# Softmax attention with decay, then two mixture layers, on one core: q and k rounded for both heads at once, row sums cut at other columns, and the conversions' ScalarE and GpSimd work queued a half step later

## The chip, the cores and the metric

The kernel runs on one core of a Trainium2 chip. A core has five engines that run side by side, each with its own queue that is worked off in order: TensorE (PE; its weight loads are listed as PEld), VectorE (DVE), ScalarE (ACT), GpSimd (POOL), and SyncE (SP), which here issues every DMA. Where an instruction needs what another engine makes, it waits on a semaphore, and all that stands behind it in its queue waits too. The metric is the device time of one execution in microseconds; less is better.

## The reference, cut to what matters

Four batches, eight heads, 576 tokens, 64 values a head; all in float32.

```
scores = q @ k.T / 8                                    # per batch and head, 576 x 576
decay  = cumsum(log f)[:, None] - cumsum(log f)[None]
scores = where(causal, -1e9, scores + decay)
attn   = exp(scores - max(scores, -1))
attn   = attn / (sum(attn, -1) + 1e-9)
x = attn @ v                                            # 2304 tokens x 512
h = x @ w_in;  x = (h * sigmoid(h)) @ w_out             # 512 -> 2048 -> 512
logits = x @ phi                                        # 2304 x 32 slots
d = softmax of logits over tokens; c = softmax of logits over slots
slot_input = d.T @ x
slot_out   = relu(slot_input[e] @ w1[e]) @ w2[e]        # 8 experts, 4 slots each
out = c @ slot_out
```

The two weights of the middle layer arrive as 64-bit words, which the kernel itself turns into float32 (the "conversions").

## The kernel before, in words

**Attention** (up to 215 us of the span). The 32 heads are worked in 16 pairs: `att_step(i)` is one head, `i` even is the first of a pair `p`, `i` odd the second. What a step does, and in which order, stands in the string `ORDER`, one half (ahead of and behind the `|`) for each head of a pair; a letter is a kind of work and the digit its piece. `m` (`max_piece`, lines 184 to 190) multiplies q by k for a coming head to find the row maxima: TensorE writes a bank of PSUM, VectorE reduces it. `f0` (line 203) joins the maxima, `f1` (`max_fin_b`, lines 207 to 214) has TensorE transpose them (tile `mtp`), copies the result out (`mr`, line 212) and sends it by DMA as one more row of q. `s` (`s_piece`, lines 233 to 242) multiplies again, for the scores with the maxima in them (tile `st`), and ScalarE takes the exponential (`E`, line 238); GpSimd cuts the causal triangle. `v` (`av`) multiplies by v for the pair before, `r` (`row_sums`) multiplies by ones to get the softmax's denominators for the pair before, which go by way of `RS`, `sg` and a piece of HBM `R` into `RB`, spread over partitions (`norm_b`, the letter `n`); `norm_c` (the letter `b`, line 313) multiplies the outputs by them.

q and k are needed in two pieces: rounded to the matmul's fast type (`split_hi`, the letter `q`, on ScalarE: lines 151 and 152 for q, 148 and 149 for k) and the rest (`split_lo`, the letter `z`, on GpSimd). Step `i` does both for head `i+4`, so two pairs ahead. A pair's q and k come in one DMA of 1152 KB (`load`, line 133), issued in the first head's step behind the row sums' DMAs, into one of two buffers, and are first read by ScalarE in the next pair's first step.

`mx`, `mtp` and `rs` tiles take turns in three banks of PSUM (ring `235`), `st` tiles in three others (ring `014`): a multiply waits until the tile three turns ago has been read out.

**Middle layer** (215 to 537 us). 36 steps `k`, each a chunk `c` of 256 tokens by a quarter `fg` of the hidden columns: two halves of 12 matmuls of 512 columns (`h_half`, lines 547 to 549), each followed by a tanh on ScalarE (`g_tanh`, line 562) and a product on VectorE (`g_mul`, line 569). The tiles `h` take turns in three banks. Twice in each step `conv_ops(4)` hands out conversion work from a list `CQ`: four instructions of VectorE (lines 443 to 459), and what stands between them for ScalarE (446, 466, 470) and GpSimd (477 to 482), which is counted as nothing. When a slice of `w_out` is done, `w_prime_a/b/c` transposes it (`wtp`), multiplies it by phi (`wp`) and writes it back to HBM; only then can the rows that need it be transposed (`g_tr`, tile `gtp`) and multiplied (`g_lp`, tile `lp`). `ROOM` says how many weight units may have been asked for by which step.

The lines that hand out the conversion work, and the one that starts a slice:

```
while n > 0 or (CQ and CQ[0] and CQ[0][0] == 0):      # CQ[0][0] is 1 for VectorE, 0 for the others
...
    v, fn, m = CQ.pop(0)
    n -= v
    fn(m)
...
stage[0] = mo["wp"].pop(0)[1] if mo["wp"] and mo["wp"][0][0] < k else None
```

**Tail** (537 us to the end): the slots' two expert layers and the result, whose 64 weight units stream in.

Of the kernel before, what the change touches and what calls it, by code (L numbers as in the profile page):

```python
# [9 lines left out]
F32 = mybir.dt.float32  # L10
F32R = mybir.dt.float32r
BF16 = mybir.dt.bfloat16
I32 = mybir.dt.int32
AF = mybir.ActivationFunctionType
ALU = mybir.AluOpType
AX = mybir.AxisListType

ORDER = "v0 m0 q0 v1 v2 m1 m2 s0 s1 f0 m3 q1 z0 p s2 a3 s3 m4 r s4 l0 s5 c m5 z1 f1 | q1 q0 v0 v1 s0 l1 f0 f1 s1 s2 z0 b n v2 m0 m1 v3 m2 w s3 m3 s4 z1 m4 s5 m5 a3 c"
CONV_AT = (2, 6, 10, 14, 18, 22, 28, 29)
LAST = 10  # L20
SPARE = 2
# [4 lines left out]
NW = 8  # L26
CAPS = ((0, 12), (5, 6))
LAG = 1
ROOM = ((17, 7), (20, 8), (21, 9), (22, 12), (24, 13), (25, 14), (26, 18), (27, 21), (28, 22), (32, 27), (33, 30), (34, 33), (35, 36), (36, 46))
RING_A, RING_B, RING_T = "014", "235", "b"  # L30


# [1 line left out]
def tile_attention_moe_softmoe(ctx: ExitStack, tc: tile.TileContext, qk, vr, f, wcat, phi, w1, w2, out):  # L34
    nc = tc.nc
    B, NP, DH, _, _, S = qk.shape
    NH = B * NP * 2
    NPAIR = B * NP
# [79 lines left out]
    staged = {}  # L118
    QB, KB = {}, {}

    def load(p):
        b, hp = divmod(p, NP)
        src = qk[b, hp]
        if p == 0:
            staged[p] = ([UB[:, h] for h in range(2)],
                         [att.tile([128, S], F32, name="k0", tag="k0", bufs=2) for h in range(2)])
            nc.sync.dma_start(out=UB, in_=src[:, 0])
            for h in range(2):
                nc.sync.dma_start(out=staged[p][1][h], in_=src[:, 1, h])
# [10 lines left out]
    def split_hi(i, which):  # L140
        p, h = divmod(i, 2)
        src = staged[p][which][h]
        if h == 0:
            nm, keep_in = (("QB", QB), ("KB", KB))[which]
            keep_in[p] = att.tile([128, 2, S], F32R, name=nm, tag=nm, bufs=3)
        t = (QB, KB)[which][p]
        if which:
            nc.scalar.activation(KA[p % 3][0:64, h], src[0:64], AF.Copy)
            nc.scalar.activation(t[64:128, h], src[64:128], AF.Copy)
        else:  # L150
            nc.scalar.activation(QA[p % 3][0:64, h, 64:640], src[0:64], AF.Copy)
            nc.scalar.activation(t[:, h], src, AF.Copy)  # L152

    def split_lo(i, which):
        p, h = divmod(i, 2)
        src = staged[p][which][h]
        t = (QB, KB)[which][p]
        eng = nc.vector if i < 4 and which == 1 else nc.gpsimd
# [83 lines left out]

    AVP, U, RT = {}, {}, {}
    SUMS, READY, done = set(), set(), {"r": 0, "n": 0, "b": 0}
    CUT = 384

    def row_sums(p):
        t = bank(RING_T, [128, CUT], "rs")
        for kb in range(5):
            k = 64 if kb == 4 else 128  # L250
            for half, c0, c1 in ((0, 0, CUT), (1, CUT, S)):
                q0 = max(c0, 128 * kb)
                for h in range(2):
                    g = 32 * (2 * half + h)
                    if q0 < c1:
                        nc.tensor.matmul(t[g:g + 32, q0 - c0:c1 - c0], lhsT=ones[0:k],  # L256
                                         rhs=E[2 * p + h][kb][0:k, q0 - 128 * kb:c1 - 128 * kb], start=kb == 0,
                                         stop=kb == (2, 4)[half])
# [4 lines left out]
        for half, p0, n in ((0, 0, CUT), (1, 64, S - CUT)):  # L263
            row = r[64 * half:64 * half + 1]
            src = bass.AP(tensor=row.tensor, offset=row.offset, ap=[[32 * r.ap[0][0], 2], [1, n]])
            nc.sync.dma_start(out=sg[p0:p0 + n // 6], in_=src)
# [24 lines left out]
    def norm_b(p):  # L291
        sg = RT[p]
        nc.vector.tensor_scalar(sg, sg, 1e-9, None, ALU.add)
        nc.vector.reciprocal(sg, sg)
        r = hbm.tile([2, S], F32, name="R", tag="R", bufs=2)
        for c0, c1, p0 in ((0, CUT, 0), (CUT, S, 64)):
            nc.sync.dma_start(out=r[:, c0:c1].rearrange("h (c j) -> h c j", j=12), in_=sg[p0:p0 + (c1 - c0) // 6])
        if p < NPAIR - 1:
            rb = att.tile([128, S], F32, name="RB", tag="RB", bufs=1)
        else:  # L300
            rb = xpool.tile([128, S], F32, name="RB", tag="x1", bufs=1)
        for h in range(2):
# [12 lines left out]
    def att_step(i, cv):  # L315
# [22 lines left out]
        for op in ORDER.split("|")[h].split():  # L338
# [9 lines left out]
                done["r"] += 1  # L348
            elif k == "a" and 0 <= i - 1 < NH:
                SUMS.add(i - 1)  # L350
            elif k == "q" and 0 <= i + 4 < NH:
                split_hi(i + 4, int(j))
            elif k == "z" and 0 <= i + 4 < NH:
                split_lo(i + 4, int(j))
# [528 lines left out]
    with tc.manual_schedule():  # L883
# [70 lines left out]
        def square(k):  # L954
# [104 lines left out]
```

## Time and profile before

| what | us |
|---|---|
| median of three runs | 606.86 (605.06 to 607.2) |
| the profiled execution | 606.83 |
| its span (first to last instruction) | 605.1 |
| TensorE busy | 544.5 |
| ScalarE busy | 345.0 |
| VectorE busy | 321.5 |
| GpSimd busy | 211.6 |

The profile takes one execution. A view of waits lists which engine sat idle at which line, and which engine's end released it; the chain of waits follows the work that ended last back from the end; a timeline lists instructions by their start with their duration (when instructions are pipelined, the distance to the next start is the better price); windows give busy time of each engine in a stretch, with the clock that TensorE was granted (1.00 is full speed).

### The profile page before, as it was taken

The page shows a single profiled execution, that of the slowest core. Times are in us where ns is not written, and L with a number is a line of the kernel's source. Part 1 is how long each engine was busy: PE and PEld are TensorE (multiplying, and loading weights), DVE is VectorE, ACT ScalarE, POOL GpSimd, SP SyncE. Part 2 cuts the span into 40 slices and gives each one's busy share as a digit, 9 for nine tenths or more (in the row PEclk, how much of TensorE's full clock was granted, in tenths as well). Part 3 has the DMA queues.
Part 4 walks back from the last instruction along what each step waited for, and adds up shares of the span by engine and source line. Part 5 has one row for each costly group of instructions (what it writes and reads, how often), then busy time and mean ns, then how long its engine had stood idle before and what let it go on. Part 6 is the DMA issues. An engine that isn't in the chain of part 4 may idle for free.

```text
span 605.1 us, 10940 instructions
## 1 busy us (share of the span) xinstructions
PE 544.5 (90%) x3959; PEld 375.0 (62%) x3959; DVE 321.5 (53%) x872; ACT 345.0 (57%) x783; POOL 211.6 (35%) x294
## 2 busy tenths in 40 slices
PE   3689999999999999797997999989989999978993
PEld 2456665656666677585775777757667777733542
DVE  7458667677786579888578413332342341322113
ACT  6599899988998685465554545334343342322022
POOL 6367877678877421653343600000000000002000
PEclk9999999999999999799998999999999999999998
DMA  5644445635552267421122071121233017589998
GB/s 206 213 146 159 163 165 157 225 125 175 177 156 94 85 235 293 178 85 56 70 83 92 36 278 36 36 79 61 64 141 110 0 36 275 211 279 347 348 299 260
DMA packets 44872, 94.30 MB, mean 156 GB/s; under 512 B 6642, under 2 KB 27922, under 8 KB 42898
## 3 DMA queue, kind: packets, MB, share of 16 engines
q1 hardware_dynamic: 44818, 93.61, 45.4%
q8 instruction: 31, 0.51, 0.4%
q14 instruction: 23, 0.19, 0.1%
HBM read 83.64 MB, written 9.13 MB: 153 GB/s over the span
## 4 chain that ended last, share of the span: by engine, by line
PE 66%; ACT 15%; DVE 9%; issue 4%; DMA 3%; POOL 1%; SPq 0%; ACTq 0%; DVEq 0%; POOLq 0%
PE h L547 9%; PE h L548 8%; PE h L549 8%; PE gtp L579 6%; PE mx L184 5%; PE av L278 4%; PE st L233 3%; PE rs L256 3%; PE lp L588 3%; PE pp L697 3%; PE st L235 3%; PE so L826 3%; PE h L760 2%; ACT E L238 2%; DVE wt L453 2%
## 5 line engine op out<-in xcount | busy, mean ns | idle before, releaser
L547 PE MATMUL h<-w,xh 128*128 128x512 f32 x288 | 118.3, 411 | 1.1 <-DVE gt L569 1.1
L569 DVE SCALAR_TENSOR_TENSOR gt<-gt,h 128x512 f32<-128x512 f32 (+1 forms) x73 | 49.5, 679 | 128.9 <-ACT gt L562 128.9
L548 PE MATMUL h<-w,xl 128*128 128x512 f32 x288 | 114.5, 397 | 0.0
L549 PE MATMUL h<-w,xh 128*128 128x512 f32 x288 | 114.4, 397 | 0.0
L562 ACT ACTIVATE gt<-h 128x512 f32<-128x512 f32 (+1 forms) x73 | 42.7, 587 | 95.0 <-PE h L549 89.2
L190 DVE CUSTOM_DVE_ANT_0 junk<-mx,mask 128x64 bf16<-128x64 f32 (+4 forms) x160 | 65.9, 428 | 48.9 <-PE mx L184 46.6
L184 PE MATMUL mx<-KA,QA 127*128 127x256 f32 (+2 forms) x192 | 64.4, 378 | 24.4 <-ACT mr L212 9.4
L238 ACT ACTIVATE E<-st 128x256 f32<-128x256 f32 (+2 forms) x192 | 63.2, 379 | 16.1 <-PE st L235 14.9
L240 POOL TENSOR_SCALAR_AFFINE_SELECT E<-E 128x128 f32<-128x128 f32 (+1 forms) x160 | 52.9, 346 | 53.7 <-ACT E L238 51.9
L735 POOL MEMSET SM<- 128x512 f32 x2 | 1.0, 524 | 191.1 <-ACT gt L562 188.7
L184 PEld LDWEIGHTS mx<-KA,QA 127*128 127x128 f32 x192 | 36.2, 203 | 45.1 <-issue 16.8
L547 PEld LDWEIGHTS h<-w,xh 128*128 128x128 f32 x288 | 54.9, 191 | 14.2 <-DVE gt L569 2.0
L549 PEld LDWEIGHTS h<-w,xh 128*128 128x128 f32 x288 | 54.8, 190 | 13.0
L548 PEld LDWEIGHTS h<-w,xl 128*128 128x128 f32 x288 | 55.0, 191 | 11.4
L233 PE MATMUL st<-QA,KA 128*128 128x256 f32 (+1 forms) x192 | 59.9, 322 | 0.9 <-DMA QA<-mr 0.5
L278 PE MATMUL av<-E,VF 128*64 128x320 f32 (+4 forms) x448 | 60.0, 374 | 0.0
L235 PE MATMUL st<-QB,KB 128*128 128x256 f32 (+1 forms) x192 | 54.6, 299 | 0.0
L580 ACT ACTIVATE gr<-gtp 128x512 f32<-128x512 f32 x72 | 39.0, 593 | 19.6 <-PE gtp L579 19.5
L579 PE MATMUL gtp<-ident,gt 128*128 128x128 f32 x288 | 41.4, 288 | 5.4 <-ACT wT L598 3.0
L162 POOL TENSOR_TENSOR QB<-qk,QB 64x576 fp32r<-64x576 f32 x30 | 42.7, 1424 | 8.2 <-ACT QB L152 5.9
L579 PEld LDWEIGHTS gtp<-ident,gt 128*128 128x128 f32 x288 | 31.8, 144 | 18.7 <-issue 7.1
L233 PEld LDWEIGHTS st<-QA,KA 128*128 128x128 f32 x192 | 35.4, 185 | 12.2 <-ACT E L238 9.1
(146 smaller groups left out, 865.7 us busy)
## 6 DMA issues: line engine op xcount, KB each, us to landing
unit<-in_w_dram SPq DMA_DIRECT2D x64, 512.0 KB
qk<-in_qk_dram SPq DMA_DIRECT2D x15, 1152.0 KB
raw<-in_w_dram SPq DMA_DIRECT2D x32, 512.0 KB
VF<-in_v_dram SPq DMA_DIRECT2D x16, 320.0 KB
RB<-R SPq DMA_DIRECT2D x32, 144.0 KB
WO<-wt SPq DMA_DIRECT2D x8, 512.0 KB
unit<-WO SPq DMA_DIRECT2D x8, 512.0 KB
out_dram<-ob SPq DMA_DIRECT2D x16, 256.0 KB
```

Of the source, the lines that this page charges most:

```text
L184: nc.tensor.matmul(t[:, 0:n], lhsT=qa[0:127, h, 128 * blk:128 * blk + 128], rhs=ka[0:127, h, k0:k0 + n], start=True, stop=True)
L190: nc.vector.tensor_tensor_reduce(out=junk[:, 0:w], in0=t[:, 0:w], in1=mask[:, 448 - w:448], scale=1.0, scalar=-3e38, op0=ALU.add, op1=ALU.max,
L233: nc.tensor.matmul(t[0:m, 0:n], lhsT=ka[:, h, k0:k0 + m], rhs=qa[:, h, 64 + q0:64 + q1], start=True, stop=False)
L235: nc.tensor.matmul(t[0:m, 0:n], lhsT=kb_[:, h, k0:k0 + m], rhs=qb[:, h, q0:q1], start=False, stop=True)
L238: nc.scalar.activation(e[0:m, c0:c0 + n - skip], t[0:m, skip:n], AF.Exp, scale=0.125)
L240: nc.gpsimd.affine_select(out=e[0:m, 0:m], in_=e[0:m, 0:m], pattern=[[1, m]], compare_op=ALU.is_ge, fill=0.0, base=0, channel_multiplier=-1)
L278: nc.tensor.matmul(AVP[p][x][64 * h:64 * h + 64, o0:o0 + n], lhsT=VF[p % 2][0:k, kb, h], rhs=E[2 * p + h][kb][0:k, c:c + n], start=kb == 0 ...
L547: nc.tensor.matmul(o, lhsT=xh[:, d, tok], rhs=w[:, 0], start=(d == 0), stop=False)
L548: nc.tensor.matmul(o, lhsT=xl[:, d, tok], rhs=w[:, 0], start=False, stop=False)
L549: nc.tensor.matmul(o, lhsT=xh[:, d, tok], rhs=w[:, 1], start=False, stop=(d == 3))
L569: nc.vector.scalar_tensor_tensor(g, g, 1.0, h[:, n * j:n * j + n], op0=ALU.add, op1=ALU.mult)
L579: nc.tensor.transpose(tp[:, j, 128 * t:128 * t + 128], g[:, t, 128 * u:128 * u + 128], ident)
```

## The change

Four things change.

- `split_hi` takes a whole pair: q of both heads in the first head's step (letter `q0`), k of both in the second's (`q1`), with two instructions of 1152 columns for each where there were four of 576. `split_lo` follows: q's two heads in the first step, k's in the second. The first pair's k comes in one DMA in place of two.
- Row sums: the 576 queries are cut into the middle 288 and the two ends of 144, which share columns, where the cut was at 384. A pair's denominators take 22 matmuls where there were 16, one copy of 128 partitions by 288 columns where there were two, one DMA into `sg` and one into `R` where there were two each, and four DMAs into `RB` where there were two.
- The maxima `mr` are copied by VectorE in place of ScalarE.
- `conv_ops` stops as soon as its four VectorE instructions are out; what stands behind them for ScalarE and GpSimd comes at the start of the next call, a half step later. A slice's `w_prime_a` then starts one step later while conversions are under way. `ROOM` is another table.

```diff
-ORDER = "v0 m0 q0 v1 v2 m1 m2 s0 s1 f0 m3 q1 z0 p s2 a3 s3 m4 r s4 l0 s5 c m5 z1 f1 | q1 q0 v0 v1 s0 l1 f0 f1 s1 s2 z0 b n v2 m0 m1 v3 m2 w s3 m3 s4 z1 m4 s5 m5 a3 c"
+ORDER = "v0 m0 q0 v1 v2 m1 m2 s0 s1 f0 m3 z0 p s2 a3 s3 m4 r s4 l0 s5 c m5 z1 f1 | q1 v0 v1 s0 l1 f0 f1 s1 s2 z0 b n v2 m0 m1 v3 m2 w s3 m3 s4 z1 m4 s5 m5 a3 c"
-ROOM = ((17, 7), (20, 8), (21, 9), (22, 12), (24, 13), (25, 14), (26, 18), (27, 21), (28, 22), (32, 27), ...
+ROOM = ((18, 5), (22, 9), (23, 10), (26, 14), (27, 17), (28, 19), (30, 22), (32, 27), ...
...
+    def split_hi(p, which):
+        src = staged[p][which]
+        nm, keep_in = (("QB", QB), ("KB", KB))[which]
+        t = keep_in[p] = att.tile([128, 2, S], F32R, name=nm, tag=nm, bufs=3)
+        if which:
+            nc.scalar.activation(KA[p % 3][0:64], src[0:64], AF.Copy)
+            nc.scalar.activation(t[64:128], src[64:128], AF.Copy)
+        else:
+            nc.scalar.activation(QA[p % 3][0:64, :, 64:640], src[0:64], AF.Copy)
+            nc.scalar.activation(t, src, AF.Copy)
...
-        nc.scalar.activation(mr[0:5 * n], tp, AF.Copy)
+        nc.vector.tensor_copy(mr[0:5 * n], tp)
...
-    CUT = 384
+    CUT = 144
+    RS = [(1, 0, CUT, CUT + 288, 0, 0), (0, 0, 0, CUT, 0, 0), (1, 1, CUT, CUT + 288, 0, 0), (0, 1, 0, CUT, 0, 1),
+          (0, 0, CUT + 288, 576, CUT, 0), (1, 2, CUT, CUT + 288, 0, 0), (0, 1, CUT + 288, 576, CUT, 0),
+          (0, 2, CUT + 288, 576, CUT, 0), (1, 3, CUT, CUT + 288, 0, 1), (0, 3, CUT + 288, 576, CUT, 0),
+          (0, 4, CUT + 288, 576, CUT, 1)]
...
-        r = att.tile([128, CUT], F32, name="RS", tag="RS", bufs=1)
-        nc.scalar.activation(r[0:64], t[0:64], AF.Copy)
-        nc.scalar.activation(r[64:128, 0:S - CUT], t[64:128, 0:S - CUT], AF.Copy)
+        r = att.tile([128, S // 2], F32, name="RS", tag="RS", bufs=1)
+        nc.scalar.activation(r, t, AF.Copy)
...
-        while n > 0 or (CQ and CQ[0] and CQ[0][0] == 0):
+        while n > 0:
...
-            stage[0] = mo["wp"].pop(0)[1] if mo["wp"] and mo["wp"][0][0] < k else None
+            stage[0] = mo["wp"].pop(0)[1] if mo["wp"] and mo["wp"][0][0] < k - bool(CQ) else None
```

ScalarE in the attention, from a conversion at the end of a pair's first step into its second step, before (KA, KB, QA, QB are the rounded pieces of one head):

```order
L466 ACTIVATE w<-wt 128x512
L148 ACTIVATE KA_87<-qk 64x576
L149 ACTIVATE KB<-qk 64x576
L151 ACTIVATE QA_84<-qk 64x576
L152 ACTIVATE QB<-qk 128x576
L238 ACTIVATE E<-st 128x256
L212 ACTIVATE mr<-mtp 10x128
L238 ACTIVATE E<-st 128x320
```

The same place with the change, and on to the next pair's first step:

```order
L458 ACTIVATE w<-wt 128x512
L143 ACTIVATE KA_87<-qk 64x1152
L144 ACTIVATE KB<-qk 64x1152
L232 ACTIVATE E<-st 128x256
L232 ACTIVATE E<-st 128x320
L232 ACTIVATE E<-st 128x448
L276 ACTIVATE UB<-av 128x320
L232 ACTIVATE E_1124<-st 128x320
L232 ACTIVATE E_1124<-st 128x192
L232 ACTIVATE E_1124<-st 64x64
L462 ACTIVATE raw<-raw 128x512
L146 ACTIVATE QA_85<-qk 64x2x576
```

The second step now rounds k of both heads and no q, and `mr` has left the queue; q of both heads comes as two long instructions in the next first step.

VectorE where the maxima of a pair are joined, before (`x` are the normed outputs, `sg` the row sums, `junk` the mask sums of which the maxima are kept):

```order
L203 TENSOR_TENSOR Mt<-Mt,Mx 128x2
L313 TENSOR_TENSOR x_94<-UB,RB 128x256
L313 TENSOR_TENSOR x_95<-UB,RB 128x256
L313 TENSOR_TENSOR x_102<-UB,RB 128x64
L293 TENSOR_SCALAR sg<-sg 96x12
L294 RECIPROCAL sg<-sg 96x12
L190 ISA junk,Mt<-mx,mask 128x64
```

And with the change:

```order
L197 TENSOR_TENSOR Mt<-Mt,Mx 128x2
L206 CAST mr<-mtp 10x128
L305 TENSOR_TENSOR x_94<-UB,RB 128x256
L305 TENSOR_TENSOR x_95<-UB,RB 128x256
L305 TENSOR_TENSOR x_102<-UB,RB 128x64
L284 TENSOR_SCALAR sg<-sg 96x12
L285 RECIPROCAL sg<-sg 96x12
L184 ISA junk,Mt<-mx,mask 128x64
```

The copy, which waits for TensorE's transpose, stands ahead of the three products and of all that follows them.

ScalarE in the middle layer around the fourth pair of converted `w_in` slices, before (`w` rounds a converted slice, `wt` and `raw` are conversion steps, `gt` the tanh, `wT` and `gr` read transposes out, `arena` a result of `w_prime_c`):

```order
L466 ACTIVATE w<-wt 128x512 x2
L562 ACTIVATE gt<-h 128x512
L446 ACTIVATE wt<-wt,nbias 128x512 x2
L562 ACTIVATE gt<-h 128x512
L616 ACTIVATE arena<-wp_3781 128x64
L598 ACTIVATE wT<-wtp 128x512 x2
L580 ACTIVATE gr<-gtp 128x512 x2
L470 ACTIVATE raw<-raw 128x512 x2
```

And with the change:

```order
L458 ACTIVATE w<-wt 128x512 x2
L554 ACTIVATE gt<-h 128x512
L598 ACTIVATE small<-wp_3785 128x256
L438 ACTIVATE wt<-wt,nbias 128x512 x2
L462 ACTIVATE raw<-raw 128x512 x2
L554 ACTIVATE gt<-h 128x512 x2
L608 ACTIVATE arena<-wp_3842 128x64
L590 ACTIVATE wT<-wtp 128x512 x2
L572 ACTIVATE gr<-gtp 128x512 x2
```

`w` and the `wt` behind it stand a half step later against VectorE's work, and the slice's transposes a step later. VectorE's own conversion instructions keep their places; on TensorE the slices and rows come one step later from step 4 on until step 30, and the same from there to the end.

## Rows read from the trace of the kernel before

**Rows 1.** The page: shares of the chain that ended last, by engine.
```profile
PE 66%; ACT 15%; DVE 9%; issue 4%; DMA 3%; POOL 1%; SPq 0%; ACTq 0%; DVEq 0%; POOLq 0%
```

**Rows 2.** Windows: stretch, length; busy by engine; clock, DMA share, GB/s.
```profile
40.00:215.00 175.00, 164.77 (x1393) 109.21 (x1391) 122.59 (x416) 152.32 (x372) 128.12 (x204) 1.00 0.46 152
219.00:345.00 126.00, 113.24 (x566) 88.35 (x565) 96.56 (x174) 69.83 (x136) 51.89 (x40) 0.95 0.34 128
345.00:535.00 190.00, 185.11 (x1177) 132.32 (x1176) 61.17 (x157) 75.00 (x167) 2.22 (x2) 1.00 0.31 110
```

**Rows 3.** Timeline of ScalarE, 90 to 98 us: start, duration, engine, line.
```profile
90.18 0.48 ACT L260 ACTIVATE RS<-rs 64x384 f32<-64x384 f32 x1 [0.47 <-ACT E L238]
90.69 0.33 ACT L261 ACTIVATE RS<-rs 64x192 f32<-64x192 f32 x1
91.04 0.43 ACT L238 ACTIVATE E<-st 128x192 f32<-128x192 f32 x2
...
92.81 0.68 ACT L149 ACTIVATE KB<-qk 64x576 fp32r<-64x576 f32 x1
93.50 0.68 ACT L151 ACTIVATE QA<-qk 64x576 fp32r<-64x576 f32 x1
94.09 0.67 ACT L152 ACTIVATE QB<-qk 128x576 fp32r<-128x576 f32 x1
...
94.93 0.25 ACT L212 ACTIVATE mr<-mtp 10x128 fp32r<-10x128 f32 x1
...
97.00 0.68 ACT L151 ACTIVATE QA<-qk 64x576 fp32r<-64x576 f32 x1
```

**Rows 4.** Waits, 40 to 215 us: total, times, longest.
```profile
PE mx L184 <- ACT mr L212: 9.4, 13, 1.1
...
ACT QA L151 <- DMA qk<-in_qk_dram: 5.4, 5, 2.4
```

**Rows 5.** Timeline of TensorE, a row-sum stretch.
```profile
112.78 1.76 PE L256 MATMUL rs<-E,ones 128*32 128x384 f32 x32
```

**Rows 6.** Timeline of SyncE and ScalarE: two loads of q and k, one read.
```profile
91.93 0.41 SPq L133 DMA_DIRECT2D qk<-in_qk_dram  x1
...
116.42 0.41 SPq L133 DMA_DIRECT2D qk<-in_qk_dram  x1
...
123.71 0.69 ACT L151 ACTIVATE QA<-qk 64x576 fp32r<-64x576 f32 x1 [2.37 <-DMA qk<-in_qk_dram]
```

**Rows 7.** Timeline of three engines, 153.7 to 158.5 us.
```profile
153.90 2.25 DVE L313 TENSOR_TENSOR x<-UB,RB 128x256 f32<-128x256 f32 x3
...
154.67 0.27 PE L210 MATMUL mtp<-ident,Mt 128*10 128x128 f32 x1
...
154.48 1.59 POOL L160 TENSOR_TENSOR KB<-qk,KA 64x576 fp32r<-64x576 f32 x1
...
157.97 0.49 DVE L190 CUSTOM_DVE_ANT_0 junk<-mx,mask 128x320 bf16<-128x320 f32 x1 [0.99 <-PE mx L184]
```

**Rows 8.** Waits, 215 to 345 us.
```profile
DVE gt L569 <- ACT gt L562: 23.2, 16, 4.0
ACT wt L446 <- DVE wt L443: 22.5, 10, 4.6
...
PE wtp L597 <- POOL wt L482: 4.9, 3, 2.3
```

**Rows 9.** Windows of the three stalls in the conversions, columns as above.
```profile
240.00:260.00 20.00, 15.92 (x65) 11.96 (x66) 17.33 (x31) 10.20 (x19) 9.61 (x6) 0.83 0.42 172
280.00:300.00 20.00, 16.49 (x92) 13.09 (x92) 14.61 (x25) 11.57 (x23) 6.23 (x6) 0.91 0.21 79
320.00:340.00 20.00, 15.70 (x94) 11.88 (x93) 13.06 (x20) 8.72 (x18) 9.11 (x8) 0.91 0.14 58
```

**Rows 10.** Timelines of ScalarE and TensorE in the second stall.
```profile
284.15 1.33 ACT L446 ACTIVATE wt<-wt,nbias 128x512 int32<-128x512 int32 x2 [1.77 <-DVE wt L443]
...
286.62 1.97 PE L579 MATMUL gtp<-ident,gt 128*128 128x128 f32 x8 [2.42 <-ACT wT L598]
```

More of the change, by code (lines that the diff above doesn't have):

```diff
@@ L28 @@
 LAG = 1
-ROOM = ((17, 7), (20, 8), (21, 9), (22, 12), (24, 13), (25, 14), (26, 18), (27, 21), (28, 22), (32, 27), (33, 30), (34, 33), (35, 36), (36, 46))
+ROOM = ((18, 5), (22, 9), (23, 10), (26, 14), (27, 17), (28, 19), (30, 22), (32, 27), (33, 30), (34, 33), (35, 36), (36, 46))
 RING_A, RING_B, RING_T = "014", "235", "b"
@@ L124, in load @@
         if p == 0:
[L125 to L129, printed above, removed]
+            staged[p] = UB, att.tile([128, 2, S], F32, name="k0", tag="k0", bufs=1)
+            for c in range(2):
+                nc.sync.dma_start(out=staged[p][c], in_=src[:, c])
             return
         t = ld.tile([128, 2, 2, S], F32, name="qk", tag="qk", bufs=2)
-        staged[p] = [[t[:, c, h] for h in range(2)] for c in range(2)]
+        staged[p] = t[:, 0], t[:, 1]
         nc.sync.dma_start(out=t, in_=src)
@@ L138, in load_v, with split_lo @@
         nc.sync.dma_start(out=VF[p % 2], in_=vr[b, hp])
[L140 to L145, printed above, removed]
-        t = (QB, KB)[which][p]
[L147 to L158, printed above, removed]
+    def split_hi(p, which):
[8 more added lines that the diff above has]
+            nc.scalar.activation(t, src, AF.Copy)
+    def split_lo(p, which, h):
+        src = staged[p][which][:, h]
+        t = (QB, KB)[which][p]
+        eng = nc.vector if p < 2 and which == 1 else nc.gpsimd
         if which:
@@ L244, in tile_attention_moe_softmoe @@
     SUMS, READY, done = set(), set(), {"r": 0, "n": 0, "b": 0}
-    CUT = 384
+    CUT = 144
[3 more added lines that the diff above has]
+          (0, 4, CUT + 288, 576, CUT, 1)]
     def row_sums(p):
-        t = bank(RING_T, [128, CUT], "rs")
-        for kb in range(5):
+        t = bank(RING_T, [128, S // 2], "rs")
+        for half, kb, c0, c1, o, stop in RS:
             k = 64 if kb == 4 else 128
[L251 to L258, printed above, removed]
-        r = att.tile([128, CUT], F32, name="RS", tag="RS", bufs=1)
-        nc.scalar.activation(r[0:64], t[0:64], AF.Copy)
-        nc.scalar.activation(r[64:128, 0:S - CUT], t[64:128, 0:S - CUT], AF.Copy)
+            q0 = max(c0, 128 * kb)
+            for h in range(2):
+                g = 32 * (2 * half + h)
+                nc.tensor.matmul(t[g:g + 32, o + q0 - c0:o + c1 - c0], lhsT=ones[0:k],
+                                 rhs=E[2 * p + h][kb][0:k, q0 - 128 * kb:c1 - 128 * kb], start=kb == 0, stop=bool(stop))
+        r = att.tile([128, S // 2], F32, name="RS", tag="RS", bufs=1)
+        nc.scalar.activation(r, t, AF.Copy)
         sg = nrm.tile([96, 12], F32, name="sg", tag="sg", bufs=2)
[L263 to L266, printed above, removed]
+        nc.sync.dma_start(out=sg, in_=bass.AP(tensor=r.tensor, offset=r.offset, ap=[[32 * r.ap[0][0], 4], [1, S // 2]]))
         RT[p] = sg
@@ L294, in norm_b @@
         nc.vector.reciprocal(sg, sg)
-        r = hbm.tile([2, S], F32, name="R", tag="R", bufs=2)
-        for c0, c1, p0 in ((0, CUT, 0), (CUT, S, 64)):
-            nc.sync.dma_start(out=r[:, c0:c1].rearrange("h (c j) -> h c j", j=12), in_=sg[p0:p0 + (c1 - c0) // 6])
+        r = hbm.tile([96, 12], F32, name="R", tag="R", bufs=2)
+        nc.sync.dma_start(out=r, in_=sg)
         if p < NPAIR - 1:
@@ L302, in norm_b @@
         for h in range(2):
-            row = r[h:h + 1]
-            nc.sync.dma_start(out=rb[64 * h:64 * h + 64],
-                              in_=bass.AP(tensor=row.tensor, offset=row.offset, ap=[list(row.ap[0]), [0, 64], [1, S]]))
+            rbh, n = rb[64 * h:64 * h + 64], S // 2
+            ends = bass.AP(tensor=rbh.tensor, offset=rbh.offset, ap=[list(rbh.ap[0]), [S - CUT, 2], [1, CUT]])
+            nc.sync.dma_start(out=ends, in_=bass.AP(tensor=r.tensor, offset=r.offset + h * n, ap=[[0, 64], [CUT, 2], [1, CUT]]))
+            nc.sync.dma_start(out=rbh[:, CUT:S - CUT],
+                              in_=bass.AP(tensor=r.tensor, offset=r.offset + (2 + h) * n, ap=[[0, 64], [1, n]]))
         RT[p] = rb
@@ L350, in att_step @@
                 SUMS.add(i - 1)
[L351 to L354, printed above, removed]
+            elif k == "q" and 0 <= p + 2 < NPAIR:
+                split_hi(p + 2, h)
+            elif k == "z" and 0 <= p + 2 < NPAIR:
+                split_lo(p + 2, h, int(j))
             elif k == "f":
```

## The prediction

> **What bounds the kernel now.** I read the page first, for the engines on whose work the chain rests, then windows by stage, then the waits of each stage, and last single timelines where two engines hold each other up. TensorE holds 66% of the chain, ScalarE 15%, VectorE 9% [rows 1]. By stages there are two stretches with something to win [rows 2]. In the attention (40 to 215 us) TensorE is busy 164.8 of 175 us and ScalarE 152.3: two engines close to full, in turn. In the middle layer while weights are converted (219 to 345) TensorE lacks 12.8 us, at a mean clock of 0.95. From 345 to 535 it is busy 185.1 of 190 us, so there the change can only move work. In the attention the wait that ends last on TensorE is the maxima's copy: 13 of the pairs wait for ScalarE's `mr`, 9.4 us in all; ScalarE in turn waits for little but q and k to land, five times, 5.4 us [rows 4]. In the conversions VectorE waits for tanh (23.2 us) while ScalarE waits for VectorE's conversion instructions (22.5 us): each stands behind the other in order [rows 8].
>
> **The attention, part by part, for one pair.**
>
> Rounding. Starts lie 0.69 us apart after a k instruction and 0.59 after a q one [rows 3]. What 576 more columns cost, I take from the two copies of the sums, 0.33 us for 192 columns and 0.48 for 384 [rows 3]: 0.15/192, or 0.8 ns a column, so 0.46 us. A merged pair of instructions thus saves 0.69 - 0.46 = 0.23 us for k, 0.13 for q; two of each, 0.72 us. Bounds: nothing, if long instructions cost their 0.69 and 0.59 in proportion, and 2.56 us if the second half were free.
>
> The Trainium skill ("ScalarE: Activation LUTs", What ACT_TABLE_LOAD costs) gives an ACTIVATE with immediate operands 186 ns and 0.833 ns a column, and lets neighbours overlap by some 93 ns. By that the four instructions saved would give an estimate of 0.37 us, not 0.72. The q rows agree, the k rows lie further apart than their own duration of 0.68, so no overlap shows there, and I keep the rows' sum.
>
> Row sums' copy. Two copies take from 90.18 to 91.04, 0.86 us [rows 3]; one of 288 columns costs 0.33 + 96 x 0.0008 = 0.41, some 0.44 with its gap. Saved 0.42.
>
> Maxima. `mr` leaves ScalarE: 0.25 us saved by its duration [rows 3]. VectorE pays about 0.25 (a reduction's 0.49 for 320 columns [rows 7] is the upper end, nothing the lower), and TensorE's 9.4/13 = 0.7 us wait for that bank goes, since the transpose is done long before ScalarE gets to it.
>
> So ScalarE is relieved of 0.72 + 0.42 + 0.25 = 1.4 us a pair. With about 14 pairs in full swing that would be 19 us if ScalarE alone set the pace. Three things eat most of it.
>
> First, the load of q and k. It was issued at 91.93 and first read at 97.00 [rows 3, 6], without a wait but 5.1 us after; another, issued at 116.42, held ScalarE for 2.37 us until 123.71, 7.3 us after [rows 6]. The load stands in SyncE's queue behind the sums' copy and its DMAs, of which one is dropped (0.4 us earlier, by the load's own issue); but ScalarE comes to q earlier by all that it is relieved of. So pairs that now just make it will wait some 0.5 us, and the five that wait already win next to nothing, the more as the merged q stands whole behind that load (2 x (0.59 + 0.46) = 2.1 us in front of the first exponential, where 1.2 stood).
>
> Second, VectorE. The copy waits for the transpose, which starts at 154.67 in a pair whose products start at 153.90 [rows 7]; it ends some 0.3 us later, so the products start 1.2 to 1.3 us later. Behind them VectorE had 0.99 us of slack before the third reduction [rows 7]; that is used up, and 0.3 us are late in such a pair. The products take 2.25 us here because a long GpSimd instruction runs beside them (1.59 us from 154.48 [rows 7]); the later they start, the less of that they meet.
>
> The Trainium skill ("GPSIMD Engine Reference", Specifications) says that GpSimd shares its SBUF interfaces with VectorE instructions that have two SBUF inputs, as these products do; the row agrees, and the rule lets me expect a second half of the products at undisturbed speed.
>
> Third, the row sums on TensorE: 22 matmuls where there were 16, in four column groups side by side, the longest with 800 columns where it had 832. The stretch takes 1.76 us for 32 entries [rows 5], 0.055 an entry: by columns it becomes 1.69, by entries (44) 2.42. I take 0.2 us more, nearer to the columns, since a pair's sums run beside each other.
>
> The DMAs (sums: two fewer, `RB`: two more) hide beside everything, as the products read `RB` half a pair later; without that cover they would cost VectorE two issues, 0.8 us a pair. The first pair's k in one DMA moves the same bytes in a start that waits for the decays, so it costs nothing.
>
> Of 1.4 us and the 0.7 of the bank, which lie one behind the other only in part, I take 0.4 us a pair as what comes through: 14 x 0.4 = 5.6 us. Bounds: 19 us won, or 0.3 + 0.66 us a pair lost, 13 us.
>
> **The conversions.** VectorE's conversion work and its order stay; ScalarE's and GpSimd's share comes half a step later, and with it a slice's transposes come one step later. Before, ScalarE reaches a `wt` when VectorE has just been given what it waits for, and the tanh and the read-outs stand behind: at 284.15 after 1.77 us of waiting, then 1.33 us of its own, and TensorE stands 2.42 us for the `wT` behind it [rows 10]. With the change about half of these waits (those for the last of four VectorE instructions) find their input ready; the ones in the middle of a call remain. The first stall is another one: TensorE's next work is to transpose a slice that GpSimd is still making, 4.9 us in three waits, 2.3 the longest [rows 8], and a step later that slice is done.
>
> What there is to win: in three windows TensorE lacks 4.1 + 3.5 + 4.3 = 11.9 us, and the granted clock is 0.83, 0.91 and 0.91, worth 3.4 + 1.8 + 1.8 = 7.0 us more [rows 9]: 18.9 us at most. The 0.83 is a mean of the two levels, 2.4 GHz and, for a third of that window, 1.2; TensorE had idled for 4.1 us of it. What is late next is VectorE: in 240 to 260 it is busy 17.3 of 20 us, 13.1 to 14.6 in the others [rows 9]. I take the first stall without its second half and a third of the two others, 2.3 + 1.7 (clock) + 2.5 = 6.5 us. Bounds: nothing (the stall moves to VectorE), or a loss of 6 us if a slice that comes a step later starves the rows, which then stall TensorE as often as now; and 18.9 won. The rows moved out of this stretch are done by step 30, beside a TensorE that is full, and cost what they cost now. `ROOM` asks for fewer units between steps 17 and 30 and for as many from 32 on; the tail's loads stay where they are.
>
> **The sum.** The profiled execution took 606.83 us, 1.7 beyond its span, and the median is 606.86, the same. 606.8 - 5.6 - 6.5 = 594.7; I say 595.
>
> **Rivals.**
>
> A: the load of q and k becomes the pace of the attention. For it: 5.1 us from issue to first read with no room to spare, five waits now [rows 4, 6]. Against it: the load also leaves earlier. Then about 1 us is won there in all, and the conversions' 6.5: 599.
>
> B: the conversions are bound by VectorE, and each stall only changes its name. For it: 17.3 of 20 us in the first window; against it: 13.1 in the third [rows 9]. Then only the attention's 5.6: 601.
>
> C, on the other side: VectorE becomes the bound of the attention. In every pair the copy `mr` waits at the head of VectorE's queue for a transpose that stands behind two multiplications by v and one for scores; products, sums and six reductions stand behind it, and TensorE's banks wait for those. It decides from 0.99 us of delay on [rows 7], which 1.25 us passes. At 0.3 us, and 0.2 for the row sums' additional entries, 14 pairs lose 7 us; with 3 won in the conversions 611. Against it: everything ahead of the transpose moves forward too.
>
> D: both halves come in nearly whole, since the two engines held each other: 1 us a pair and 9 us in the conversions, 584.
>
> That the change doesn't do what it says I give nothing of its own: the orders show the moves.
>
> **How the numbers follow.** Forecast 0.45, A 0.20, B 0.13, C 0.12, D 0.10. The range: 587 to 606. Below lies most of D, above C; A and B are within. What can be told from no change is 0.5%, 3 us, so 603.8 and 609.9 are the borders: faster takes the forecast, D and most of A and B, 0.79; a tenth is left for a result within them; slower 0.11.
>
> **What would show it.** Right: the period of the pairs (loads of q and k) falls from (116.42 - 91.93)/2 = 12.2 us [rows 6] to under 12; the wait of `mx` for `mr` is gone; waits of ScalarE for q and k grow in number; the waits of `wtp` for GpSimd and of `wt` for VectorE shrink, and the three windows lack less than 6 us together. Wrong: a new wait of TensorE's `mx` for VectorE of 0.3 us a pair or more (C), the row-sum stretch at over 2.2 us, or a stall in the conversions as long as now at another place (B).

## The result, and the profile after

The changed kernel takes 590.96 us (median of four runs, 589.63 to 591.87), the kernel before 606.91 beside it; the ratio is 0.974, its 95% interval 0.972 to 0.977. The profiled execution spans 589.2 us against 605.1, 15.9 less. By TensorE's timelines that splits into three: the middle layer's first product starts at 215.05 us and not at 219.31 (-4.3), the stretch from there to the last `lp` is 304.5 us long and was 318.4 (-14.0), and the tail takes 69.7 us where it took 67.4 (+2.3).

The page's chain by engine, as [rows 1] had it before:

```profile
PE 75%; DVE 9%; ACT 6%; DMA 5%; issue 3%; POOL 1%; SPq 0%; ACTq 0%; DVEq 0%; POOLq 0%
```

ScalarE's 15% are 6%, and transfers stand on the chain with 5%. The stages of [rows 2] and the three stalls of [rows 9], windows of the kernel after in the same columns (stretch, length; TensorE, weight loads, VectorE, ScalarE, GpSimd; clock, DMA share, GB/s):

```profile
40.00:215.00 175.00, 170.53 (x1619) 116.20 (x1616) 114.81 (x435) 141.69 (x303) 126.41 (x206) 1.00 0.51 154
219.00:345.00 126.00, 121.69 (x658) 93.92 (x657) 109.05 (x175) 75.59 (x148) 58.04 (x40) 1.00 0.40 148
...
240.00:260.00 20.00, 17.46 (x87) 13.48 (x86) 20.00 (x29) 9.45 (x18) 11.55 (x9) 1.00 0.38 154
...
280.00:300.00 20.00, 20.00 (x112) 15.35 (x111) 19.00 (x29) 10.28 (x19) 11.08 (x8) 1.00 0.33 106
320.00:340.00 20.00, 19.38 (x126) 14.78 (x125) 9.59 (x14) 10.15 (x22) 4.88 (x4) 1.00 0.49 185
```

The stalls are nearly gone: the three windows lack 2.5 + 0.0 + 0.6 = 3.1 us where they lacked 11.9, and the granted clock is 1.00, the 2.4 GHz level, throughout. VectorE is busy for all 20 us of the first. What is left there is one wait; the waits from 215 to 345 us (total, times, longest) answer to [rows 8]:

```profile
ACT wt L438 <- DVE wt L435: 15.0, 8, 3.1
DVE gt L561 <- ACT gt L554: 13.8, 8, 6.1
ACT raw L462 <- DVE raw L449: 8.9, 5, 4.5
...
PE h L539 <- DVE gt L561: 2.5, 1, 2.5
```

TensorE's wait for a slice that GpSimd makes (4.9 us) isn't among them any more; ScalarE's wait of `raw` for VectorE has grown from 1.2 us. In the attention (40 to 215 us, to [rows 4]):

```profile
ACT RS L255 <- PE rs L252: 19.5, 14, 1.4
...
DVE mr L206 <- PE mtp L204: 15.5, 14, 1.1
...
ACT QA L146 <- DMA qk<-in_qk_dram: 7.1, 8, 1.8
...
PEld mx L178 <- DVE Mx L181: 5.0, 13, 0.4
```

TensorE no longer waits for `mr`. ScalarE now has time over in every pair: it waits 14 times, 1.4 us each, for the row sums. One pair in a timeline (start, duration, engine, line; to [rows 3, 5 to 7]):

```profile
88.65 0.46 SPq L131 DMA_DIRECT2D qk<-in_qk_dram  x1
88.83 1.16 ACT L143 ACTIVATE KA<-qk 64x1152 fp32r<-64x1152 f32 x1
88.84 1.41 POOL L156 TENSOR_TENSOR QB<-qk,QB 64x576 fp32r<-64x576 f32 x1
89.95 0.28 DVE L206 CAST mr<-mtp 10x128 fp32r<-10x128 f32 x1 [1.10 <-PE mtp L204]
90.01 1.16 ACT L144 ACTIVATE KB<-qk 64x1152 fp32r<-64x1152 f32 x1
90.16 0.89 DVE L305 TENSOR_TENSOR x<-UB,RB 128x256 f32<-128x256 f32 x3
...
94.08 1.17 ACT L146 ACTIVATE QA<-qk 64x1152 fp32r<-64x1152 f32 x1 [0.73 <-DMA qk<-in_qk_dram]
95.16 1.15 ACT L147 ACTIVATE QB<-qk 128x1152 fp32r<-128x1152 f32 x1
...
97.51 1.78 PE L252 MATMUL rs<-E,ones 128*32 128x288 f32 x44
99.41 0.41 ACT L255 ACTIVATE RS<-rs 128x288 f32<-128x288 f32 x1 [1.43 <-PE rs L252]
99.76 0.43 ACT L232 ACTIVATE E<-st 128x192 f32<-128x192 f32 x2
...
100.53 0.46 SPq L131 DMA_DIRECT2D qk<-in_qk_dram  x1
```

Read it as a loop: the load issued at 88.65 is waited for at 94.08; behind the rounding come the exponentials, the row sums, their copy, its transfer, and then the next load at 100.53. Twelve loads from 40.93 to 173.36 us lie 12.04 us apart, 12.42 before (42.23 to 178.85); without the last step, which is 13.2 us long, 11.93. The chain of waits between 40 and 205 us shows what this loop weighs, before and after (shares by line):

```profile
by line: PE mx L184 15.3%; PE av L278 11.9%; PE rs L256 10.1%; PE st L233 9.0%; PE st L235 7.6%; ACT E L238 7.3%; issue 5.1%; ACT QA L151 4.8%; ACT KB L149 4.5%; ACT QB L152 4.5%; DMA qk<-in_qk_dram 4.0%; ACT w L466 2.3%; DVE junk L190 2.2%
```

```profile
by line: PE av L269 20.8%; PE mx L178 14.2%; PE rs L252 14.1%; PE st L227 13.6%; DMA qk<-in_qk_dram 10.1%; PE st L229 8.8%; issue 4.9%; ACT QB L147 3.1%; ACT E L232 2.2%; ACT UB L274 2.1%; DVE junk L184 1.3%; ACT RS L255 0.7%; DVE wt L445 0
```

ScalarE's rounding (QA, KB and QB 13.8% together) is 3.1%, and the load has gone from 4.0% to 10.1%. The tail's 2.3 us are lost in its first 20 us, while the experts' weights stream in; two windows just behind the last `lp`, before and after, each with the same group of TensorE's from a timeline:

```profile
538.00:558.00 20.00, 15.08 (x144) 6.12 (x144) 5.00 (x19) 4.13 (x21) 3.61 (x8) 0.91 1.07 347
...
548.14 4.09 PE L870 MATMUL si<-unit,arena 128*32 128x512 f32 x32 [0.47 <-ACT arena L863]
```

```profile
520.00:540.00 20.00, 15.07 (x102) 6.35 (x104) 5.00 (x19) 2.16 (x7) 1.51 (x3) 0.74 1.09 350
...
529.93 6.40 PE L862 MATMUL si<-unit,arena 128*32 128x512 f32 x32 [0.47 <-ACT arena L855]
```

TensorE is busy as long in both, and idle for 4.9 us, but the mean clock is 0.74 and not 0.91: a longer share at the 1.2 GHz level, in which the same 32 multiplications take 6.40 us and not 4.09. The tail's code is the same in all fourteen kernels profiled here, and its length goes with this clock: 67.1 to 67.9 us in the seven traces with 0.91, 68.0 to 68.7 in six with 0.83, 69.7 in this one. The conversions alone have 0.91, the attention alone has 0.91 with the old `ROOM` and 0.83 with the new, so nothing ties the loss to one of the edits. Why an execution gets one clock or another was not tried.

### The profile page after: what moved, and what is told of

It reads as the page before. It is cut to its first block, busy times and chain, and to the rows that moved or that the text cites. A ratio compares the mean times of both kernels' runs of the same rounds, so it can differ in the third digit from the quotient of the medians.

```text
span 589.2 us, 11255 instructions
## 1 busy us (share of the span) xinstructions
PE 542.8 (92%) x4151; PEld 377.2 (64%) x4151; DVE 320.7 (54%) x889; ACT 327.5 (56%) x686; POOL 214.0 (36%) x294
## 4 chain that ended last, share of the span: by engine, by line
PE 75%; DVE 9%; ACT 6%; DMA 5%; issue 3%; POOL 1%; SPq 0%; ACTq 0%; DVEq 0%; POOLq 0%
PE h L539 9%; PE h L541 9%; PE h L540 9%; PE av L269 7%; PE gtp L571 6%; PE mx L178 5%; PE rs L252 5%; PE st L227 5%; PE st L229 3%; PE lp L580 3%; PE pp L689 3%; DMA qk<-in_qk_dram 3%; PE so L818 3%; PE h L752 2%; DVE wt L445 2%
## 5 line engine op out<-in xcount | busy, mean ns | idle before, releaser
L539 PEld LDWEIGHTS h<-w,xh 128*128 128x128 f32 x288 | 54.1, 188 | 16.4 <-DVE gt L561 4.4
L541 PEld LDWEIGHTS h<-w,xh 128*128 128x128 f32 x288 | 54.1, 188 | 12.8
L571 PE MATMUL gtp<-ident,gt 128*128 128x128 f32 x288 | 40.2, 282 | 3.9 <-ACT gr L572 2.3
```

The costliest lines, as they stand in the source:

```text
L539: nc.tensor.matmul(o, lhsT=xh[:, d, tok], rhs=w[:, 0], start=(d == 0), stop=False)
L541: nc.tensor.matmul(o, lhsT=xh[:, d, tok], rhs=w[:, 1], start=False, stop=(d == 3))
L571: nc.tensor.transpose(tp[:, j, 128 * t:128 * t + 128], g[:, t, 128 * u:128 * u + 128], ident)
```

## The experiments

All ratios are to the kernel before on the same chip, with 95% intervals; the kernel after stands at 0.974 (0.972 to 0.977). "First `h`" and "stretch" are the start of the middle layer and its length to the last `lp`, as above (before 219.3 and 318.4, after 215.1 and 304.5); both are read from one profiled execution of each kernel.

| kernel | median us | ratio (95%) | first `h` | stretch |
|---|---|---|---|---|
| attention alone | 604.89 | 0.995 (0.993 to 0.997) | 215.0 | 320.4 |
| the same, new `ROOM` | 604.54 | 0.995 (0.993 to 0.998) | 217.5 | 319.6 |
| conversions alone | 593.37 | 0.976 (0.973 to 0.979) | 219.4 | 306.3 |
| after, no half-step delay | 596.59 | 0.982 (0.979 to 0.986) | 214.7 | 312.3 |
| after, slices not a step later | 595.88 | 0.981 (0.978 to 0.985) | 217.3 | 311.3 |
| after, old row sums | 595.20 | 0.979 (0.976 to 0.982) | 219.6 | 304.7 |
| after, rounding split by head | 592.48 | 0.976 (0.972 to 0.981) | 217.0 | 304.5 |
| after, `mr` on ScalarE | 591.35 | 0.975 (0.969 to 0.980) | 214.7 | 306.0 |
| after, early load | 599.58 | 0.987 (0.984 to 0.990) | 225.3 | 304.9 |
| after, early load, late sums | 601.72 | 0.991 (0.988 to 0.994) | 228.6 | 306.1 |
| after, late sums | 602.66 | 0.990 (0.987 to 0.994) | 229.8 | 304.8 |
| after, load in two halves | 585.83 | 0.965 (0.963 to 0.967) | 208.4 | 306.0 |

**One half each.** The changed kernel with the conversions of before, `ROOM` included:

```diff
+ROOM = ((17, 7), (20, 8), (21, 9), ...      # as before
-        while n > 0:
+        while n > 0 or (CQ and CQ[0] and CQ[0][0] == 0):
-... mo["wp"][0][0] < k - bool(CQ) else None
+... mo["wp"][0][0] < k else None
```

> The change's attention edits alone (rounding by pairs, row sums, maxima on VectorE), with the conversions and ROOM as before. Theory (the two halves of the change add up, and the attention gives what the shift of the first matmul of the middle layer shows, 219.31 to 215.05 us): 606.9 - 4.3 = 602.6 us, first middle-layer matmul at 215 us, stalls at 243 to 249, 281 to 287 and 320 to 327 us as before, each 4 us earlier. Rival (most of the gain needs both halves, since the conversions start at another distance from the loads): under 598 or over 606.

The other half: the kernel before with the two edits of the conversions and the new `ROOM`, its attention untouched.

> The change's conversion edits alone (conv_ops stops at four, slices a step later, the new ROOM) on the attention as before. Theory: the rest of the gain, about 11.5 us: 595.4 us, first middle-layer matmul at 219.3, TensorE short of 5 us or less from 219 to 345 us at a granted clock of 1.00. Rival (the conversions' gain comes from the attention's earlier end or from the new ROOM's loads): 600 or more.

Conversions alone bring 2.4%, 14.4 us by the medians; the attention alone 0.5%, 2.9 us, though its first `h` comes as early as in the changed kernel: in that trace 2 us of the 4.3 are lost again in a stretch whose stalls are still there. How far one first `h` can be trusted: five kernels of the table have the changed attention as it is (after, both with the attention alone, both of the conversions' parts below), and theirs lie at 214.7, 215.0, 215.1, 217.3 and 217.5. In the two late ones a load behind 160 us takes 7.5 and 8.1 us until ScalarE goes on. So a difference of 2 us between two traces decides nothing.

`mr` back on ScalarE:

```diff
-        nc.vector.tensor_copy(mr[0:5 * n], tp)
+        nc.scalar.activation(mr[0:5 * n], tp, AF.Copy)
```

> The changed kernel with the maxima copied by ScalarE again; all else as changed. Theory (the pair's pace is set by the load of q and k, and the copy's move only takes TensorE's wait of 0.7 us from a place that has slack): 591 to 594 us, with TensorE's mx waiting for mr again in most pairs. Rival 1 (the move is what the attention's gain rests on): 595 us. Rival 2 (VectorE's wait at the head of its queue, 15.5 us in 14 pairs, costs more than the copy's move saves): below 590.

It costs nothing that can be told. That TensorE would wait for `mr` again was expected, and it doesn't: from 40 to 215 us this is all that its multiplications wait for.

```profile
PE st L227 <- ACT E L232: 2.4, 5, 1.1
```

So the 9.4 us of [rows 4] did not go because VectorE makes the copy. The transpose and the copy of one pair, with the copy on ScalarE, and below them the transpose that belongs to the copy at 94.93 of [rows 3]:

```profile
90.66 0.27 PE L204 MATMUL mtp<-ident,Mt 128*10 128x128 f32 x1
92.48 0.25 ACT L206 ACTIVATE mr<-mtp 10x128 fp32r<-10x128 f32 x1
```

```profile
92.00 0.27 PE L210 MATMUL mtp<-ident,Mt 128*10 128x128 f32 x1
```

ScalarE comes to the copy 1.8 us behind the transpose's start and not 2.9; those 1.1 us are the longest wait of [rows 4]. The likely reason is that the rest of the change has shortened ScalarE's queue; no run isolates it.

**Parts of the attention.** `row_sums` and `norm_b` as before (cut at 384, two copies, two transfers into `sg`):

```diff
-    CUT = 144
+    CUT = 384
-        nc.scalar.activation(r, t, AF.Copy)
+        nc.scalar.activation(r[0:64], t[0:64], AF.Copy)
+        nc.scalar.activation(r[64:128, 0:S - CUT], t[64:128, 0:S - CUT], AF.Copy)
...
```

> The changed kernel with the row sums as before (cut at 384, two copies, two DMAs into sg and R, two into RB). Theory (the sums' copy and the DMA behind it stand in the loop load, q, products, row sums, copy, load, so 0.42 us of copy and one DMA of 0.6 us come back in every pair): 12 to 13 pairs x 0.8 = 10 us at most, some 5 us after what the later stages give back: 594 to 599. Rival (more matmuls cost what the shorter copy gains): 589 to 592.

The long rounding instructions cut in two, in the same places:

```diff
-            nc.scalar.activation(KA[p % 3][0:64], src[0:64], AF.Copy)
...
+        for h in range(2):
+                nc.scalar.activation(KA[p % 3][0:64, h], src[0:64, h], AF.Copy)
...
```

> The changed kernel with each long rounding instruction of 1152 columns split into two of 576, in the order head 0, head 1; places in the order as changed. Theory (each split costs 0.13 to 0.23 us of ScalarE, 0.26 us for q stand in the load's loop): 0.3 us in 13 pairs, 4 us at most, some 2 us after the middle layer: 591 to 595. Rival (the merged form is what pays, 0.72 us a pair): 598 or more.

With the old sums the whole gain of the attention is gone (219.6, loads 12.37 us apart): one more copy and one more transfer stand ahead of each load. With the rounding split the loads lie 12.17 us apart over ten steps (41.42 to 163.09), against 11.93 in the changed kernel; in the time its interval holds the kernel after. What these parts have in common is the loop, and its share on the chain of the split kernel says so, 17.5% for the load:

```profile
by line: DMA qk<-in_qk_dram 17.5%; PE rs L253 12.8%; PE av L270 12.5%; PE st L228 9.8%; PE mx L179 8.6%; ACT E L233 6.3%; PE st L230 5.9%; issue 5.1%; ACT QB L148 4.9%; ACT QA L147 3.7%; ACT KA L144 2.3%; ACT KB L145 2.0%; ACT RS L256 2.0%;
```

**Parts of the conversions.** The changed kernel with the loop condition of before:

```diff
-        while n > 0:
+        while n > 0 or (CQ and CQ[0] and CQ[0][0] == 0):
```

> The changed kernel with conv_ops handing out ScalarE's and GpSimd's pieces at once again; slices still start a step late and ROOM is the new one. Theory (the conversions' gain of 13 us rests for the larger part on the half step's delay, which lets tanh and the read-outs go ahead of pieces that wait for VectorE): 599 to 603 us, ScalarE's waits for VectorE's wt back at 20 us or more from 215 to 345. Rival (it rests on the slices' later start, which spares TensorE the waits for GpSimd): 591 to 595.

And with a slice's transposes a step earlier:

```diff
-... mo["wp"][0][0] < k - bool(CQ) else None
+... mo["wp"][0][0] < k else None
```

> The changed kernel with the slices' transposes started as early as before the change (threshold k instead of k - bool(CQ)); the half step's delay stays. Theory (GpSimd's last pieces now come half a step later, so TensorE's transposes would wait for them): 595 to 600 us, with waits of wtp for GpSimd's wt of 8 us or more, at three or more places. Rival (the later start matters little, since the stall of wtp was 4.9 us in all before): 591 to 592.

The delay is worth 7.8 us of the stretch, the later slices 6.8; in the time, by the ratios, some 5 and 4 us, with intervals of 2 us on either side. 599 to 603 us had been expected without the delay, 596.59 came. Over the 126 us from the first `h` TensorE is idle for 12.8 us before, 4.3 after, 9.6 without the delay and 8.1 with early slices. In the three windows of [rows 9] TensorE lacks 5.0, 0.7 and 0.5 us with the delay alone, and 3.4, 1.2 and 1.8 with the later slices alone: only both together clear the first stall. Without the delay the waits of 215 to 345 us show ScalarE held by VectorE's conversions again, twice as long as after, and TensorE held in turn:

```profile
ACT wt L438 <- DVE wt L435: 31.2, 12, 6.1
...
PE h L539 <- DVE gt L561: 7.0, 4, 3.4
```

With early slices it is TensorE's wait for GpSimd that is back, and the first stall stands as it stood [rows 9], clock 0.83 included:

```profile
PE wtp L589 <- POOL wt L474: 6.9, 4, 3.0
```

```profile
240.00:260.00 20.00, 15.04 (x64) 11.50 (x64) 16.17 (x27) 8.98 (x16) 8.90 (x7) 0.83 0.46 181
```

The table `ROOM` was tried on the attention-alone kernel:

```diff
-ROOM = ((17, 7), (20, 8), (21, 9), ...
+ROOM = ((18, 5), (22, 9), (23, 10), ...
```

> The change's attention edits with the conversions as before and only the new table ROOM. Theory (ROOM spares pages for the later releases and costs or gains nothing itself): as the attention edits with the old table, ratio to before 0.993 to 0.997. Rival (fewer unit loads between steps 17 and 30 account for a part of the conversions' gain): 0.990 or less.

604.54 against 604.89, the same ratio: no effect there. The changed conversions with the old table weren't tried, so a share of the new table in their 14.4 us is not excluded by a run.

**The load.** If it closes the loop, an earlier one should help. First, `l0` moved ahead of the sums' transfers:

```diff
-ORDER = "... z0 p s2 a3 s3 m4 r s4 l0 s5 c m5 z1 f1 | ...
+ORDER = "... z0 p l0 s2 a3 s3 m4 r s4 s5 c m5 z1 f1 | ...
```

> The changed kernel with the load of the next pair's q and k put ahead of the row sums' DMAs in SyncE's queue (letter l0 right behind p); nothing else. Theory (with the change, the load issued behind the row sums' copy paces the attention: load 5.4 us, q's rounding, multiplications, row sums, copy, load again): ScalarE's 8 waits for q and k (7.1 us from 40 to 212) go to under 2 us, the pairs come 0.3 to 0.6 us closer, 13 pairs: 584 to 588 us. Rival (another chain is as long, ScalarE's or TensorE's own work, or the earlier load only waits for its buffer): 590 to 592, as the changed kernel.

It loses some 8 us against the changed kernel (0.987 against 0.974), and yet ScalarE's waits for q and k are gone. The chain between 60 and 95 us shows the price:

```profile
62.22 1.76 PE rs L252 x36
64.06 0.41 ACT RS L255
64.49 5.89 DMA sg<-RS
70.40 0.22 DVE sg L284
```

The sums' transfer of 4.5 KB, issued 2.1 us behind the load of 1152 KB (and 2.9 behind 512 KB of weights), takes 5.89 us until it is read, and VectorE's queue, with the maxima that TensorE's banks wait for, stands behind it. Two attempts to move the sums (`n` and `w`) out of the way, behind the second step's maxima, with the early load and without:

```diff
-... s1 s2 z0 b n v2 m0 m1 v3 m2 w s3 m3 s4 z1 m4 s5 m5 a3 c"
+... s1 s2 z0 b v2 m0 m1 v3 m2 s3 m3 s4 z1 m4 s5 m5 n w a3 c"
```

> The changed kernel with the load of q and k ahead of the row sums' DMAs, and VectorE's work on the sums (letter n, and the load of v behind it, w) at the end of the second step. Theory (the early load alone lost 10 us in the attention because the sums' small DMA then queues behind 1152 KB, 4 to 6 us, and VectorE's maxima stand behind the instruction that waits for it; with that instruction moved behind the maxima, neither load nor sums pace the pair): first middle-layer matmul at 209 to 213 us, 584 to 589 us. Rival 1 (the sums still arrive too late for the next products, or the maxima's row, which is a small DMA too, waits behind the load): 592 or more. Rival 2 (ScalarE and TensorE's own work is as long as the load's loop): 590 to 592.

> The changed kernel with VectorE's work on the sums (n, w) at the end of the second step, the load where the change has it. Theory (the load's loop sets the pace and the sums come in time, 1.0 us of waits in all): 590 to 592 us, as the changed kernel. Rival (the sums' wait matters as soon as it is there): below 589.

Both fail. Late sums alone, with the load where it was, cost some 10 us (0.990 against 0.974); the ten executions scatter from 595.08 to 607.98, and the profiled one took 604.45. In it the load itself is late at two places of the attention. The one issued at 52.72 lets ScalarE go on at 60.41; TensorE has stood for 2.59 us, and its row sums then take 3.24 us, at a mean clock of 0.73 from 64 to 80 us:

```profile
52.72 0.46 SPq L131 DMA_DIRECT2D qk<-in_qk_dram  x1
...
60.41 1.16 ACT L146 ACTIVATE QA<-qk 64x1152 fp32r<-64x1152 f32 x1 [2.46 <-DMA qk<-in_qk_dram]
...
63.21 0.63 PE L227 MATMUL st<-QA,KA 128*128 128x320 f32 x1 [2.59 <-ACT E L232]
...
64.28 3.24 PE L252 MATMUL rs<-E,ones 128*32 128x288 f32 x44
```

The next load is issued 16.0 us behind this one, not 12, and the same happens behind a load at 160.26. On the chain from 40 to 205 us loads of q and k hold 12.8%, the maxima's 5 KB, which stands behind a load too, 3.2%. Loads as late stand in two traces above whose attention is as in the changed kernel, so what the new order adds is open.

The last experiment leaves the order alone and issues each load as two, q first:

```diff
-            nc.sync.dma_start(out=t, in_=src)
+        for c in range(2):
+            nc.sync.dma_start(out=t[:, c], in_=src[:, c])
```

> The changed kernel with each load of the loop (l0 for p above 0) issued as two transfers of 576 KB, the queries' half first, the keys' behind it on the same queue. Theory (in the changed kernel the load of 1152 KB, 5.4 us on the chain from issue to landing, then the rounding of q, the multiplies, the row sums and their copy pace the attention's pairs): the queries' half lands some 1.5 to 2.5 us earlier and the keys are wanted only half a pair later. ScalarE's waits for qk between 40 and 212 us fall from 7.1 us to under 3 us, the loads follow each other by 11.5 to 11.9 us instead of 12.04, the middle layers' first product starts at 209 to 213 us instead of 215.05, and the time is 585 to 590 us. Rival 1 (the loop is closed by another chain as long, VectorE's mr or the row sums themselves): the waits for qk fall, the period stays at 12.0, 590 to 592 us. Rival 2 (the row sums' small transfers, which queue behind a load, come later or the extra issue costs SP time): waits of the multiplies for Mt or of VectorE for sg of over 4 us in all, 592 to 598 us.

585.83 us (583.67 to 586.26): 1.0% below the changed kernel by the ratios, whose intervals don't meet. ScalarE's wait for q and k is not on its list of waits any more, the loads lie 11.61 us apart (40.25 to 167.93, twelve), the first `h` comes at 208.4, and the chain from 40 to 205 us holds no transfer:

```profile
by line: PE av L270 30.3%; PE mx L179 20.2%; PE st L228 18.3%; PE rs L253 14.7%; PE st L230 13.7%; PE mtp L205 0.9%; ACT QA L147 0.7%; ACT QB L148 0.6%; issue 0.4%; DVE junk L185 0.4%; DVE Mt L185 0.1%
```

```profile
40.00:215.00 175.00, 174.78 (x1642) 121.56 (x1639) 123.05 (x452) 145.64 (x311) 126.07 (x206) 1.00 0.54 163
```

TensorE is busy for all but 0.2 of 175 us: it alone is the bound there now. The load had closed the loop.

## Why the prediction came out as it did

595 us was forecast and 591 came, by two sizes that were off in opposite ways: 5.6 us for the attention, of which 4.3 came and 2.9 are left when that half stands alone, and 6.5 for the conversions, which brought 14.0 (alone 14.4 by the medians, 12.1 by the stretch of its trace). That the sum came within 4 us is in part luck: the conversions were off by 7.5 us, and the attention and the tail gave back 3.6 of it.

*ScalarE's relief* was sized well. KA to KB is 1.18 us from start to start, QA to QB 1.08, so a merged pair saves 2 x 0.69 - 1.18 = 0.20 and 2 x 0.59 - 1.08 = 0.10 [rows 3], 0.60 us for the four against 0.72 forecast; the sums' copy takes 0.35 to the next start in place of 0.86, 0.51 against 0.42; with `mr`'s 0.25 that is 1.36 us, forecast 1.4. The Trainium skill ("ScalarE: Activation LUTs", What ACT_TABLE_LOAD costs) gives 1.15 us as an estimate for 1152 columns, and the rows show 1.15 to 1.17; its overlap of neighbours shows for q (0.09 us) and for k not (start to start is longer than the duration).

*What eats it.* The first of the three, the load, did so nearly alone: waits for q and k went from five to eight, as foretold, and the loop paces the pairs at 12.04 us, 11.93 without the last step, about the 12 named. So the mechanism was rival A's, at a price in between: A allowed 1 us for the attention. The forecast treated the load as a wait that takes some pairs' gain; the last experiment shows that it closed the loop for them all. The second, `mr` at the head of VectorE's queue, waits as foretold (1.1 us, 14 times) and costs nothing: `mx` waits 5.0 us for VectorE, above the 0.3 us a pair named as a sign of C, but it did before the change, and does with `mr` back on ScalarE, for the same 5.0 us and 13 times, and so it isn't C. That the products would meet less of GpSimd came true: `QB` ends at 90.25, and the three from 90.16 take 0.89 us where [rows 7] had 2.25. In the kernel before itself the three take 2.14 to 2.30 us in the pairs where such a GpSimd instruction runs beside them for 1.6 us, and 1.03 in three where it does for 0.1. The Trainium skill's shared SBUF interfaces ("GPSIMD Engine Reference", Specifications) agree. The third, 0.2 us for the row sums, was nothing: 44 entries take 1.78 us, 32 took 1.76 [rows 5]; the price by entries (2.42) was the wrong one.

*The 0.7 us of the bank* was put to the wrong cause. The 9.4 us of waits for `mr` [rows 4] went, but not by VectorE's copy: with the copy back on ScalarE they stay away, since ScalarE now comes to it in time, and the kernel takes 591.35. The reading "ScalarE in turn waits for little but q and k" also left out 8.3 us, 14 times, for scores (`st`), its longer wait.

*The conversions' 6.5* was the step that failed most, by its two discounts. "The first stall without its second half and a third of the two others" assumed that waits in the middle of a call remain and VectorE is late next. The three windows got back 8.8 of 11.9 us of idle time and all 7.0 of clock; the stretch as a whole is shorter by 14.0, so some 2 us are late elsewhere in it. The two edits add up in the stretch (7.8 + 6.8 us), though not stall by stall: the first went only with both. VectorE does become full (20.0 of 20 us), as B had it, but at the end of what there was to win. The bound of a loss by starved rows did not show.

*The tail* was taken as untouched, and its code is; the 2.3 us go with the clock that the profiled execution was granted there, which differs between kernels without regard to the edits.

## What to carry to other kernels

When an engine is relieved, look for the loop that closes next, transfers included: here a load's 5.4 us from issue to landing (88.65 to 94.08), 4% of the chain before, took most of a relief of 1.4 us a pair, and cutting it by first use was worth 5 us. Two engines that wait for each other in order (ScalarE for VectorE's conversion, VectorE for ScalarE's tanh) are parted by handing one of them its work a half step later, which by itself left 1.2 us of the 7.8 of the second and third stall here; the first went only with the slices a step later as well. A small transfer behind a large one on the same queue took here 4.1 to 5.9 us against 3.0 at most ahead of it; where it carries something urgent, it goes first. And a wait that is gone after a change is only explained when the part that should have ended it is undone and the wait comes back: here it didn't.

## What the runs showed of the hardware that was not expected

The sums' 4.5 KB transfer takes 4.1 to 5.9 us at the five places where it stands on the chain with the early load, issued 1.9 to 2.7 us behind 1152 KB (in four of them behind 512 KB of weights too), and at most 3.0 ahead of that load (issued at 99.85 in the kernel after, read without a wait at 102.84). The same load of 1152 KB took 5.4 us until it was read in one pair and 7.5 and 8.1 us in traces with the same attention. Multiplications by ones in four column groups took as long with 44 entries as with 32 (1.78 and 1.76 us), so entries were not their price.
